# Start slots of the last two scans and the spacing of the first expert weights in a linear attention and two-MoE kernel

## The chip, the cores and the metric

The kernel runs on one core of one Trainium2 chip. The metric is the device time of one execution in microseconds (us). Engines are named TensorE (PE in the profile, PEld for its weight loads), VectorE (DVE), ScalarE (ACT), GpSimd (POOL) and SyncE (SP, which issues the plain DMAs).

## What is computed

Three stages follow each other. In the reference (cut to its core):

```python
for t in range(S):
    state = alpha[:, :, t, :, None] * state + einsum('bhd,bhe->bhde', k[:, :, t], v[:, :, t])
    y[:, :, t] = einsum('bhd,bhde->bhe', q[:, :, t], state)
x = y.transpose(0, 2, 1, 3).reshape(B * S, H * D)          # 3072 tokens x 384
h = x @ w_in;  x = maximum(0.01 * h, h) @ w_out            # 384 -> 2048 -> 384
expert = argmax(x @ w_gate, 1)                             # one of 8 experts for each token
out[t] = gate_prob[t] * (maximum(x[t] @ w1[expert[t]], 0) @ w2[expert[t]])
```

Here B = 4, H = 8, S = 768 and D = 48. The expert weights w1 and w2 are 8 x 384 x 1024 and 8 x 1024 x 384 in float32.

## The kernel before

**Units.** The 3072 tokens are worked on in NU = 8 units of UT = 384 tokens. For a unit, the attention makes the tile xT (the tokens' activations, turned, as a float16 high part and low part), and `moe1` runs the first MoE layer on it. The attention of unit u runs beside `moe1` of units u-2 and u-1.

**Slots.** From unit 1 on the order of the instructions on all engines is written out by hand. `moe1(u)` is a generator that yields 34 times for a unit. Each yield is a slot. In its first half there are 16 slots, one for each block f of 128 hidden columns: nine matmuls (L824), a scaled copy on ScalarE (L833), the leaky maximum on VectorE (L834), the high half on ScalarE (L839) and the low half on GpSimd (L840). In its second half there are 18 slots, mostly of nine matmuls (L847) each. `state["at"]` holds u + f/40 in the first half and u + 0.5 in the second. After each slot `run_slots` steps a list of side generators, and a side generator that yields w is stepped again w slots later.

**Side generators.** They stand in this order, and the instructions of a slot are issued in this order too:

- `full_tiles` (in the last unit alone): the routing of unit 6, then the table of the first NA = 14 expert tiles (`tile_table`, VectorE, L1010 to L1072), then a loop over j that issues the gather of tile j (an indirect DMA from GpSimd, L1303) and turns tile j - LAG (six transposes, L1316, and one ScalarE copy to XT, L1317). LAG is 6.
- `fronts`: for each unit from 2 on, `front`: transposes of alpha (L316), copies to the tile Ft (L521), six levels of a scan along the time axis (L541, two VectorE multiplications for each level), logarithms and exponentials, and the scaled k and q (L578). A start value of `state["at"]` for each unit sets when it begins: units 2 to 5 begin at slot 12 of the unit two before, unit 6 at slot 7 of unit 4, and unit 7 at slot 0 of unit 5.
- `backs`: `back(u)` follows when `front(u)` and `back(u-1)` are done: scores (L675), states (L654), outputs (L703 and L711), xh (L726) and the transposes to xT (L731). For units 2 and 7 its argument `fast` makes two of its pauses shorter.
- `first_weights`: after the last `back`, the attention's memory is given up and the expert weights of the first of four phases are loaded.
- `routed(u)`: the routing of unit u in the second half of unit u+1: small VectorE operations (L941 to L963), two matmuls (L966, L967) and three scatters of the rows (L990).

**Weight pieces.** `load_phase` splits a phase into 16 pieces of 384 KB, w1 and w2 of eight experts in turn. A piece comes by one DMA (L1100) into one of RING = 3 buffers wr. For phase 0, ScalarE squares it (L189, for a check of the range), VectorE rounds it to float16 (L1120) and then makes the low half (L1078). For phase 1, the rounding is done by ScalarE (L1118). A buffer is free when the low half is made, and then the transfer of the third piece after it is issued. The first unit's experts need all w1 pieces of phase 0. Phase 1 puts its w1 into the memory of w_in, so its first eight pieces can be written from the second half of the last unit on, and the rest follows beside the experts.

**After unit 7.** `stage(0)` and `stage(1)` copy an expert's w1 on VectorE (L1342), and then the expert steps begin (L1371, L1397).

Of the kernel before, what the change touches and what calls it, by code (L numbers as in the profile page):

```python
# [29 lines left out]
NU = NTOK // UT  # L30
# [19 lines left out]
C2 = C1 / (2.0 * SW * SW)  # L50
EXPM = 0x7F800000
RING = 3
LAG = 6
AHEAD = (0, 0, 0)
AHEAD2 = 3
WARM = (45,2,2,6,4)
# [17 lines left out]
def tile_kernel(ctx, tc, q, k, v, alpha, w_in, w_out, w_gate, w1, w2, out):  # L74
# [72 lines left out]
    parts, at = [], 2 * P  # L147
# [37 lines left out]
    def squares(src, scrap, scale=1.0):  # L185

        i = sq_n[0]
        sq_n[0] += 1
        A.activation(scrap, src, AF.Square, scale=scale, accum_out=g_sq[:, i : i + 1])  # L189
# [81 lines left out]
    state = {"S": None, "SU": None, "e": None, "nat": 0, "sm": 0, "wo": 0, "half": -1, "turned": -1, "at": 0, "attn": 1, "front": 1}  # L271
# [804 lines left out]
    def after(f):  # L1076

        f() if late is None else late.append(f)  # L1078

    def place(ph):  # L1080

        W1 = wi.tile([P, 2, E, 3, FQ], F16, tag="wi", name="W1") if ph % 2 else pw.tile([P, 2, E, 3, FQ], F16, name="W1")
        Wp[ph] = [W1, None]

    def load_phase(ph, pieces):

        raws = []
        NP = len(pieces)

        def start(n):  # L1090
            e, which = pieces[n]
            raw = pw.tile([P, 2 * DM], F32, tag="wr", name="wr", bufs=RING)
            f0 = ph * FQ
            if which == 0:
                raw = raw.rearrange("p (k f) -> p k f", k=3)
                src = w1[e, :, f0 : f0 + FQ].rearrange("(k p) f -> p k f", p=P)
            else:
                raw = raw.rearrange("p (i d) -> p i d", i=2)
                src = w2[e, f0 : f0 + FQ, :].rearrange("(i p) d -> p i d", p=P)
            nc.sync.dma_start(out=raw, in_=src)  # L1100
            raws.append(raw)

        def scaled(n):
            if n < NP and ph >= 2:
                G.tensor_scalar(raws[n], raws[n], SW, 1.0, ALU.mult, ALU.mult)  # L1105

        for n in range(min(RING, NP)):
            start(n)
        scaled(0)
        for n in range(NP):  # L1110
            scaled(n + 1)
            yield 0.0
            e, which = pieces[n]
            raw, hi, lo = raws[n], *(Wp[ph][which][:, a, e] for a in range(2))
            if ph < 2:
                squares(raw, lo.bitcast(BF16), SW)
                if ph:
                    A.activation(hi, raw, AF.Copy, scale=SW)  # L1118
                else:
                    V.tensor_scalar(hi, raw, SW, None, ALU.mult)  # L1120
                after(partial(V.scalar_tensor_tensor, lo, raw, SW, hi, ALU.mult, ALU.subtract))
            else:
                A.copy(hi, raw)
                squares(raw, lo.bitcast(BF16))
                G.tensor_tensor(out=lo, in0=raw, in1=hi, op=ALU.subtract)  # L1125
            if n + RING < NP:
                start(n + RING)
            yield 1.4
# [99 lines left out]

    def fronts():
        for u in range(2, NU):  # L1230
            while state["at"] < u - 2 + (12, 12, 12, 12, 12, 12, 7, 0)[u] / 40:
                yield 1
            yield from first_front if u == 2 else front(u, False)
            state["front"] = u
            yield 1
# [16 lines left out]
    ALL = [(e, which) for e in range(E) for which in range(2)]  # L1252
# [3 lines left out]
    def first_weights():  # L1256

        nonlocal pw
        while state["attn"] < NU - 1:
            yield 1  # L1260
        pl_ctx.close()
        pa_ctx.close()
        pw = pw_ctx.enter_context(tc.tile_pool(name="pw", bufs=1, side="right", reuse_waits="tile"))
        XT.extend(pw.tile([P, 2, 3, P], F16, name=f"XT{j}") for j in range(NA))
        acc.extend(pw.tile([P, XR], F32, name=f"acc{j}") for j in range(NA))
        sth.extend(pw.tile([P, 2, 3, FQ], F16, name=f"st{i}") for i in range(2))
        place(0)
        Wp[0][1] = pw.tile([P, 2, E, 2, DM], F16, name="W2")
        n = 0
        for _ in load_phase(0, ALL):  # L1270
            n += 1
            if n == 1:
                yield 2
            if n % 2 == 0:
                yield 1
        while state["at"] < NU - 0.5:
            yield 1
        place(1)
        for n, _ in enumerate(load_phase(1, ALL[0::2])):
            yield 1 - n % 2  # L1280

    halves = fronts(), backs()
    sides = [[0, g] for g in (*halves, first_weights())]

    def attention_done(u):
# [26 lines left out]
    def turn(j):  # L1312
        px = pst("a").bitcast(F16)
        x16 = acc[j][:, 0:DM].bitcast(F16)
        for kk in range(6):
            T.transpose(px[:, kk * P : (kk + 1) * P], x16[:, kk * P : (kk + 1) * P], ident16)  # L1316
        A.copy(XT[j].rearrange("p a k t -> p (a k t)"), px[:, 0 : 2 * DM])  # L1317

    def full_tiles():
# [4 lines left out]
        yield 1  # L1324
        for j in range(NA + LAG):
            if j < NA:
                gather(j)
                reg(V, j)
            if j >= LAG:
                turn(j - LAG)  # L1330
            yield 1
# [3 lines left out]
    def reg(eng, j):  # L1335
        if (eng, j) not in regs:
            regs[eng, j] = eng.value_load(ej[0:1, j : j + 1], min_val=0, max_val=E - 1)
        return regs[eng, j]
# [416 lines left out]
```

## Time and profile before

| | |
|---|---|
| median of 3 runs | 891.19 us (889.4 to 894.12) |
| the profiled execution | 887.91 us |
| its span | 885.8 us, mean granted clock 0.972 |
| TensorE busy | 815.1 us (92%) |
| VectorE busy | 636.7 us (72%) |
| ScalarE busy | 515.9 us (58%) |
| GpSimd busy | 466.5 us (53%) |
| chain that ended last | PE 60%, DVE 11%, ACT 8%, issue 3% |

The page gives for each engine its busy time and share of the span, and the chain of work that ended last, followed back from the last instruction. TensorE is the engine with the highest share. The eight units can be found in the trace by the first L824 after the last L847 of the unit before: unit 1 begins at 158.94 us, unit 2 at 231.88, unit 3 at 295.12, unit 4 at 358.79, unit 5 at 435.11, unit 6 at 515.90, unit 7 at 578.60, and the experts' first matmul (L1371) at 638.69.

### The profile page before, as it was taken

The page shows a single profiled execution, that of the slowest core. Times are in us where ns is not written, and L with a number is a line of the kernel's source. Part 1 is how long each engine was busy: PE and PEld are TensorE (multiplying, and loading weights), DVE is VectorE, ACT ScalarE, POOL GpSimd, SP SyncE. Part 2 cuts the span into 40 slices and gives each one's busy share as a digit, 9 for nine tenths or more (in the row PEclk, how much of TensorE's full clock was granted, in tenths as well). Part 3 has the DMA queues.
Part 4 walks back from the last instruction along what each step waited for, and adds up shares of the span by engine and source line. Part 5 has one row for each costly group of instructions (what it writes and reads, how often), then busy time and mean ns, then how long its engine had stood idle before and what let it go on. Part 6 is the DMA issues. An engine that isn't in the chain of part 4 may idle for free.

```text
span 885.8 us, 19845 instructions
## 1 busy us (share of the span) xinstructions
PE 815.1 (92%) x7099; PEld 582.4 (66%) x7099; DVE 636.7 (72%) x1561; ACT 515.9 (58%) x1262; POOL 466.5 (53%) x511
## 2 busy tenths in 40 slices
PE   7887899989999999988997999698899999999995
PEld 4654577666776776665664675454668777777884
DVE  8899886649558559558467658846476888787774
ACT  5657666566475485465266357345838666566343
POOL 6577852454373563563364435246535078678454
PEclk9889999999999999999998999799999999999999
DMA  9654361220211222311000004603614224232121
GB/s 250 174 139 108 102 159 46 54 54 25 58 28 46 63 43 60 62 28 32 24 2 0 28 19 133 193 27 103 189 48 126 91 91 126 92 126 90 66 90 66
DMA packets 130632, 72.21 MB, mean 82 GB/s; under 512 B 102954, under 2 KB 123526, under 8 KB 130528
## 3 DMA queue, kind: packets, MB, share of 16 engines
q1 hardware_dynamic: 125376, 56.64, 24.3%
q0 software_dynamic: 5152, 14.23, 4.7%
q8 instruction: 61, 1.00, 0.5%
q14 instruction: 43, 0.35, 0.1%
HBM read 62.17 MB, written 10.25 MB: 82 GB/s over the span
## 4 chain that ended last, share of the span: by engine, by line
PE 60%; DVE 11%; ACT 8%; issue 3%; POOL 1%; DMA 1%; POOLq 0%; DVEq 0%; ACTq 0%
PE m L847 14%; PE a L1371 12%; PE m L824 12%; PE m L1397 11%; DVE Ft L541 2%; PE a L316 2%; PE a L675 2%; DVE gf L834 2%; PE a L654 2%; ACT gf L833 2%; DVE W L1078 1%; PE a L703 1%; ACT sm L695 1%; ACT W L189 1%; PE a L627 1%
## 5 line engine op out<-in xcount | busy, mean ns | idle before, releaser
L847 PE MATMUL m<-woh,gh 128*128 128x392 f16 x1152 | 210.1, 335 | 1.1 <-POOL gh L840 0.8
L824 PE MATMUL m<-xT,wih 128*128 128x384 f16 x1152 | 203.9, 331 | 2.8 <-DVE gf L834 2.8
L840 POOL TENSOR_TENSOR gh<-gf,gh 128x384 f16<-128x384 f32 x128 | 124.8, 981 | 123.2 <-ACT gh L839 107.1
L847 PEld LDWEIGHTS <-gh 128*128 128x128 f16 x1152 | 113.6, 100 | 74.3 <-issue 5.3
L824 PEld LDWEIGHTS <-wih 128*128 128x128 f16 x1152 | 113.0, 100 | 74.5 <-issue 8.3
L834 DVE SCALAR_TENSOR_TENSOR gf<-m,gf 128x384 f32<-128x384 f32 x128 | 70.8, 554 | 99.2 <-ACT gf L833 98.8
L1371 PE MATMUL a<-XT,st 128*128 128x128 f16 x2016 | 132.4, 220 | 8.1 <-DVE st L1342 7.6
L1371 PEld LDWEIGHTS <-st 128*128 128x128 f16 x2016 | 121.2, 99 | 24.6 <-DVE st L1342 14.4
L1397 PE MATMUL m<-W,hs 128*128 x672 | 127.2, 326 | 0.0
L833 ACT ACTIVATE gf<-m 128x384 f32<-128x384 f32 x128 | 62.4, 489 | 64.7 <-PE m L824 62.9
L839 ACT CAST gh<-gf 128x384 f16<-128x384 f32 x128 | 65.4, 511 | 53.2 <-DVE gf L834 52.0
L1397 PEld LDWEIGHTS <-hs 128*128 128x128 f16 x672 | 61.2, 98 | 29.2
L1342 DVE COPY st<-W 128x1536 f16 x112 | 73.1, 653 | 6.6 <-POOL W L1125 4.3
L1379 ACT ACTIVATE hs<-a 128x256 f16<-128x256 f32 x112 | 42.6, 381 | 59.7 <-PE a L1371 58.6
L1383 DVE SCALAR_TENSOR_TENSOR hs<-a,hs 128x256 f16<-128x256 f32 x112 | 47.2, 422 | 36.9 <-ACT hs L1379 36.5
L990 POOL DMA_INDIRECT x_rows<-xg,pi x24 | 29.0, 1208 | 78.0 <-DVE xg L984 23.6
L1125 POOL TENSOR_TENSOR W<-wr,W 128x768 f16<-128x768 f32 x32 | 53.4, 1670 | 26.0 <-ACT W L189 19.6
L189 ACT ACTIVATE W<-wr 128x768 bf16<-128x768 f32 x64 | 54.0, 844 | 7.8 <-DMA wr<-in_moe_w 7.7
L1412 DVE SCALAR_TENSOR_TENSOR acc<-m,acc 128x384 f32<-128x384 f32 x84 | 51.7, 615 | 6.8 <-PE m L1397 0.7
L316 PE MATMUL a<-ident,nat 128*128 128x128 f32 x288 | 44.6, 289 | 9.5 <-DMA nat<-in_alpha 4.5
L1105 POOL TENSOR_SCALAR wr<-wr 128x768 f32<-128x768 f32 x32 | 33.6, 1050 | 28.7 <-DMA wr<-in_moe_w 28.5
L690 POOL TENSOR_TENSOR sh<-sm,sh 128x512 f16<-128x512 f32 x36 | 44.6, 1260 | 7.3 <-ACT sh L686 7.2
(262 smaller groups left out, 1405.2 us busy)
## 6 DMA issues: line engine op xcount, KB each, us to landing
wr<-in_moe_w SPq DMA_DIRECT2D x64, 384.0 KB, 3.1
raw_in<-in_moe_w_in SPq DMA_DIRECT2D x12, 512.0 KB, 4.3
raw<-in_moe_w_out SPq DMA_DIRECT2D x16, 384.0 KB, 3.6
nat<-in_alpha SPq DMA_DIRECT2D x24, 192.0 KB, 3.5
nat<-in_k SPq DMA_DIRECT2D x24, 192.0 KB, 3.4
nat<-in_q SPq DMA_DIRECT2D x24, 192.0 KB, 3.5
vt<-in_v SPq DMA_DIRECT2D x24, 192.0 KB, 3.7
acc<-x_rows,off POOLq DMA_INDIRECT x28, 3.5
```

The source lines that it names most:

```text
L189: A.activation(scrap, src, AF.Square, scale=scale, accum_out=g_sq[:, i : i + 1])
L316: T.transpose(pt[:, c * P : (c + 1) * P], nt[:, c, pr].rearrange("p z d -> p (z d)"), ident)
L824: T.matmul(ph[:, 0:UT], wih[:, a, kk, f * P : (f + 1) * P], xT[:, b, kk, :], start=(n == 0), stop=(n == 8),)
L833: A.activation(gf, ph[:, 0:UT], AF.Copy, scale=0.01 * CG)
L834: V.scalar_tensor_tensor(gf, ph[:, 0:UT], CG, gf, ALU.mult, ALU.max)
L839: A.copy(g[f][:, 0], gf)
L840: G.tensor_tensor(out=g[f][:, 1], in0=gf, in1=g[f][:, 0], op=ALU.subtract)
L847: T.matmul(po[:, 0:ROW], g[f][:, a, c * P : (c + 1) * P], woh[:, b, f, :], start=(n == 0), stop=(n == 3 * NF - 1),)
L1125: G.tensor_tensor(out=lo, in0=raw, in1=hi, op=ALU.subtract)
L1342: V.tensor_copy(out=sth[i % 2].rearrange("p a k f -> p a (k f)"), in_=Wp[ph][0][:, :, ds(reg(V, j), 1), :, :].rearrange("p a e k f -> p a ...
L1371: T.matmul(hp[:, f * P : (f + 1) * P], st[:, a, kk, f * P : (f + 1) * P], XT[j][:, b, kk, :], start=(n == 0), stop=(n == 8),)
L1397: T.matmul(yp[:, 0:DM], hs[:, a, i, :], W2[:, b, ds(rp, 1), i, :].rearrange("p e f -> p (e f)"), start=(n == 0), stop=(n == 5),)
```

## The change

```diff
@@ -50,7 +50,7 @@
-LAG = 6
+LAG = 5
@@ def fronts():
         for u in range(2, NU):
-            while state["at"] < u - 2 + (12, 12, 12, 12, 12, 12, 7, 0)[u] / 40:
+            while state["at"] < u - 1.7:
                 yield 1
@@ def first_weights():
-        n = 0
-        for _ in load_phase(0, ALL):
-            n += 1
-            if n == 1:
+        for n, _ in enumerate(load_phase(0, ALL)):
+            if n == 0:
                 yield 2
-            if n % 2 == 0:
-                yield 1
+            elif n % 2 == 0:
+                yield 1 if n % 4 or state["at"] > NU - 0.5 else 2
+                while NU - 1 <= state["at"] < NU - 0.9:
+                    yield 1
+                if state["at"] < NU - 0.5 and state["at"] > NU - 1:
+                    yield 3
         while state["at"] < NU - 0.5:
             yield 1
         place(1)
         for n, _ in enumerate(load_phase(1, ALL[0::2])):
-            yield 1 - n % 2
+            if n % 2:
+                yield 1 + (n % 8 == 7)
```

`front` of units 6 and 7 now begins at slot 12 of units 4 and 5, as for the other units. `back(7)` therefore ends at slot 20 of unit 6 and not at slot 8, and the first weight piece is worked on at slot 22 of unit 6 and not at slot 10. The pieces of phase 0 came one for each slot, at slots 10 to 25 of unit 6. Now eight come in slots 22 to 32 of unit 6, two for each three slots. Two come in the first half of unit 7, at slots 7 and 11, and six at its slots 16 to 23. The eight pieces of phase 1 came in slots 17 to 31 of unit 7, one for each two slots. Now they come in slots 23 to 31, one for each slot with one slot left out. The turn of a tile comes five slots after its gather, so that the last turn falls into the last slot of unit 7. No instruction is added or taken away, but for the order.

How the order moves, at three places. First VectorE in unit 5, around its scan (Ft is the tile that L541 scans, gf the leaky maximum of the first half, sm the scores). Before:

```order
L834 SCALAR_TENSOR_TENSOR gf<-m,gf 128x384
L541 TENSOR_TENSOR Ft<-Ft 128x12x32 x2
L681 COPY_PREDICATED sm_116<-tri,a 128x512
L681 COPY_PREDICATED sm_118<-tri,a 128x512
L834 SCALAR_TENSOR_TENSOR gf<-m,gf 128x384
L541 TENSOR_TENSOR Ft<-Ft 128x12x16x2 x2
L834 SCALAR_TENSOR_TENSOR gf<-m,gf 128x384
L541 TENSOR_TENSOR Ft<-Ft 128x12x8x4 x2
L834 SCALAR_TENSOR_TENSOR gf<-m,gf 128x384
L541 TENSOR_TENSOR Ft<-Ft 128x12x4x8 x2
```

and with the change, where the last L834 of unit 5 stands first:

```order
L834 SCALAR_TENSOR_TENSOR gf<-m,gf 128x384
L522 COPY a_5763<-a 128x3 x2
L541 TENSOR_TENSOR Ft<-Ft 128x12x32 x2
L719 TENSOR_REDUCE g_y<-a 128x1
L1512 TENSOR_SCALAR g_al<-g_al 128x64
L257 TENSOR_SCALAR n1m<-g_y 128x1
L1525 TENSOR_REDUCE mins<-g_al 128x1
L261 TENSOR_SCALAR n1s<-n1m 128x1
L262 TENSOR_SCALAR n1e<-n1m 128x1
L541 TENSOR_TENSOR Ft<-Ft 128x12x16x2 x2
L739 TENSOR_TENSOR xT<-a,xT 128x3x128
```

The levels of the scan stood between the L834 of the first half, and they now stand behind all of them, in the second half. With the change, VectorE's and GpSimd's orders in unit 4 are row for row those of unit 2, and in unit 5 those of unit 3, but for six small operations of a check (L1512 and the like) that were elsewhere before.

Then VectorE in unit 6, around the routing of unit 5 (W are the float16 weights, rm, rd, rsx and rex the routing's small tiles). Before:

```order
L1120 TENSOR_SCALAR W_6681<-wr 128x768
L1078 SCALAR_TENSOR_TENSOR W_6681<-wr,W_6681 128x768
L1120 TENSOR_SCALAR W_6680<-wr 128x768
L1078 SCALAR_TENSOR_TENSOR W_6680<-wr,W_6680 128x768
L941 TENSOR_REDUCE rm<-L 128x3
L943 TENSOR_TENSOR rd<-L,rm 128x24
L1120 TENSOR_SCALAR W_6681<-wr 128x768
L1078 SCALAR_TENSOR_TENSOR W_6681<-wr,W_6681 128x768
L948 TENSOR_REDUCE rsx<-rex 128x3
```

and with the change, from the end of the routing's first part to the first piece:

```order
L960 COPY rex<-con 128x8
L961 TENSOR_TENSOR rex<-rex,oh 128x8
L962 TENSOR_TENSOR rex<-rex,oh 128x8
L963 TENSOR_TENSOR con<-rex,oh 128x8
L739 TENSOR_TENSOR xT<-a,xT 128x3x128
L912 TENSOR_REDUCE mx<-m 128x1
L257 TENSOR_SCALAR n2m<-mx 128x1
L261 TENSOR_SCALAR n2s<-n2m 128x1
L262 TENSOR_SCALAR n2e<-n2m 128x1
L914 TENSOR_SCALAR L<-m,n1e 128x8
L915 SCALAR_TENSOR_TENSOR gsc<-n1e,n2e 128x1
L1120 TENSOR_SCALAR W_6864<-wr 128x768
```

The routing's operations stood between the pieces, and they now stand ahead of the first piece.

Last, ScalarE in unit 7, from the last high half (L839) on (XT are the turned tiles, L1320 is the former L1317). Before, with the pieces of phase 1 alone:

```order
L839 CAST gh<-gf 128x384
L189 ACTIVATE W_7480,g_sq<-wr 128x768
L1118 ACTIVATE W_7480<-wr 128x768
L189 ACTIVATE W_7480,g_sq<-wr 128x768
L1118 ACTIVATE W_7480<-wr 128x768
L1317 COPY XT_6650<-a 128x768
L189 ACTIVATE W_7480,g_sq<-wr 128x768
L1118 ACTIVATE W_7480<-wr 128x768
L1317 COPY XT_6651<-a 128x768
```

and with the change:

```order
L839 CAST gh<-gf 128x384
L189 ACTIVATE W_6864,g_sq<-wr 128x768
L189 ACTIVATE W_6865,g_sq<-wr 128x768
L189 ACTIVATE W_6864,g_sq<-wr 128x768
L1320 COPY XT_6834<-a 128x768
L189 ACTIVATE W_6865,g_sq<-wr 128x768
L1320 COPY XT_6835<-a 128x768
L1320 COPY XT_6836<-a 128x768
L189 ACTIVATE W_6864,g_sq<-wr 128x768
L919 ACTIVATE xg<-m,n2s 128x384
L1320 COPY XT_6837<-a 128x768
L189 ACTIVATE W_6865,g_sq<-wr 128x768
```

Six pieces of phase 0 now stand ahead of the eight of phase 1, so ScalarE has 14 pieces, 14 copies to XT and two more operations (L919) in this half where it had eight pieces.

## Rows read from the trace of the kernel before

**Rows 1.** Windows by unit: us, TensorE busy (count), granted clock, DMA share, GB/s
```profile
231.88:295.12 63.24, 63.24 (x508) 1.00 0.22 48
295.12:358.79 63.67, 63.67 (x511) 1.00 0.22 48
358.79:435.11 76.32, 70.40 (x547) 0.98 0.15 32
435.11:515.90 80.79, 72.24 (x571) 0.96 0.02 8
515.90:578.60 62.70, 53.55 (x366) 0.92 0.41 130
578.60:638.69 60.09, 54.03 (x379) 1.00 0.33 103
```
**Rows 2.** Waits of TensorE in unit 5: us in total, times, longest
```profile
PE a L316 <- DVE kt L578: 3.2, 1, 3.2
```
**Rows 3.** VectorE's scan by line: unit 3, then 4 (busy, mean ns)
```profile
L541 DVE TENSOR_TENSOR Ft<-Ft 128x384 f32<-128x384 f32 x12 | 6.1, 559 | 0.0
...
L541 DVE TENSOR_TENSOR Ft<-Ft 128x384 f32<-128x384 f32 x12 | 9.8, 868 | 0.0
```
**Rows 4.** Timeline of VectorE in unit 6, then of TensorE [idle before <-releaser]
```profile
555.88 0.96 DVE L1078 SCALAR_TENSOR_TENSOR W<-wr,W 128x768 f16<-128x768 f32 x1 [0.41 <-ACT W L189]
556.76 0.17 DVE L941 TENSOR_REDUCE rm<-L 128x3 f32<-128x24 f32 x1
...
560.58 0.59 PE L966 MATMUL a<-oh,con 128*128 128x24 f32 x2 [9.15 <-DVE rex L960]
```
**Rows 5.** Timeline of TensorE, end of unit 2: start, us, instruction
```profile
290.54 0.82 PE L316 MATMUL a<-ident,nat 128*128 128x128 f32 x6
291.20 3.65 PE L847 MATMUL m<-woh,gh 128*128 128x392 f16 x21
294.68 0.60 PE L627 MATMUL a<-ident,kt 128*128 128x128 f32 x4
295.12 1.63 PE L824 MATMUL m<-xT,wih 128*128 128x384 f16 x9
```
**Rows 6.** Line L1100, the weight pieces' transfers: unit 6, then unit 7
```profile
L1100 SPq DMA_DIRECT2D wr<-in_moe_w x16: 367/368/368, 539.4 to 572.9; - x16
...
DMA to landing us min/median/max: 2.9/3.6/5.0
...
DMA to landing us min/median/max: 3.1/3.6/4.9
```
**Rows 7.** Timeline of TensorE in unit 1, where back runs fast
```profile
218.49 0.55 PE L731 MATMUL a<-ident,xh 128*128 128x128 f32 x3 [1.66 <-ACT xh L726]
```
**Rows 8.** Timeline of ScalarE in unit 7, second half
```profile
611.50 0.84 ACT L189 ACTIVATE W<-wr 128x768 bf16<-128x768 f32 x1
...
612.34 0.83 ACT L1118 ACTIVATE W<-wr 128x768 f16<-128x768 f32 x1
613.07 0.83 ACT L189 ACTIVATE W<-wr 128x768 bf16<-128x768 f32 x1
...
614.73 0.80 ACT L1317 COPY XT<-a 128x768 f16<-128x768 f16 x1
615.42 0.85 ACT L189 ACTIVATE W<-wr 128x768 bf16<-128x768 f32 x1
```
**Rows 9.** Timeline of ScalarE, then of TensorE, end of unit 7
```profile
635.82 0.86 ACT L1118 ACTIVATE W<-wr 128x768 f16<-128x768 f32 x1
...
638.69 3.69 PE L1371 MATMUL a<-XT,st 128*128 128x128 f16 x36 [2.27 <-DVE st L1342]
```
**Rows 10.** Waits of TensorE in unit 7: us in total, times, longest
```profile
PE a L1316 <- DMA acc<-x_rows,off: 1.9, 2, 1.0
```
**Rows 11.** Timeline of VectorE, then of GpSimd, table of tiles in unit 7
```profile
602.00 2.59 DVE L1021 COPY ten<-tnt 128x8 f32<-128x8 f32 x1
...
601.90 2.65 POOL L840 TENSOR_TENSOR gh<-gf,gh 128x384 f16<-128x384 f32 x3
```

## The prediction

> **What bounds the kernel now.** I read the windows by unit first. Units 2 and 3 take 63.24 and 63.67 us, and TensorE is busy in all of it, at a granted clock of 1.00. Unit 4 takes 76.32 us, unit 5 takes 80.79 and unit 6 takes 62.70; TensorE is idle for 5.9, 8.6 and 9.2 us of them, and the granted clock is 0.98, 0.96 and 0.92 [rows 1]. So TensorE is the bound, and what can be won lies where it waits or runs at the lower of its two levels.
>
> The waits say on whom it waits. In unit 5 it waits 3.2 us on VectorE's scaling of k in a front [rows 2]. The groups by line show what makes VectorE late there: the twelve scan operations take 6.1 us in unit 3 and 9.8 in unit 4, 559 against 868 ns for one [rows 3]. In unit 6 the timeline shows one wait of 9.15 us for the routing, whose operations on VectorE stand behind the weight pieces (the piece ahead of L941 ends at 556.7) [rows 4].
>
> **Units 4 and 5.** With the change, VectorE and GpSimd have the rows of unit 2 in unit 4 and those of unit 3 in unit 5, and the attention work on TensorE is theirs too. I take their times: 63.24 for 76.32 and 63.67 for 80.79, together -30.2 us. A part of this is work that moves into unit 6 and is counted there. The bounds: no better than units 2 and 3, which have no idle time left; at worst the waits stay, which is the second rival.
>
> **Unit 6.** Against unit 2, the new unit 6 has the same TensorE work but for the 36 alpha, k and q transposes and four of the k turns. Six transposes take 0.66 us to the next row (290.54 to 291.20), so 36 take 3.96; the four turns take 0.44 [rows 5]. So unit 6 becomes 63.24 - 3.96 - 0.44 = 58.84, which is -3.9. This needs the 9.15 us wait to go, and the routing now stands ahead of the first piece. The eight pieces that follow have two for three slots of nine matmuls, which is 2.25 us for one (21 take 3.48 us there, 291.20 to 294.68, so nine take 1.5). In the run shown, 16 transfers were issued between 539.4 and 572.9, 2.2 us apart, while each waited for its buffer [rows 6], so the pieces can hold this pace. I cost them at nothing: in the second half, ScalarE and VectorE have no L833 and L834 to deliver. Were that cover gone, each would take 0.84 us of ScalarE from them (below), and from VectorE 0.96 for the low half [rows 4] and somewhat less for the rounding, some 1.5. `back(7)` runs fast here, and where `back(2)` did so, TensorE waited 1.66 us for xh [rows 7]; I take 0, since VectorE has no front beside it, and keep 1.7 for the range.
>
> Units 4 to 6 together: 219.8 before, 185.75 now, **-34.1 us**.
>
> **Unit 7.** Here the change costs. Its first half gets two pieces, 0.84 us of ScalarE and 1.5 of VectorE each. I cost them at nothing on TensorE, whose products run ahead of both by up to four buffers, but they stand ahead of the tile table on VectorE, and I add 0.4 us for the gathers that wait on it. In the second half ScalarE becomes the bound. After its last L839 a piece of phase 0 takes 0.84 us, a piece of phase 1 takes 613.07 - 611.50 = 1.57, and a copy to XT takes 615.42 - 614.73 = 0.69 [rows 8]. Up to the end of the last piece stand six, eight and twelve of these and two L919, which are smaller than a copy to XT and taken as 0.5: 5.0 + 12.6 + 8.3 + 1.0 = 26.9 us. From 611.50 this ends at 638.4. It ended at 636.55 so far (635.82, and 0.73 until the next can start), and the first expert matmul came 2.1 us later, after a wait of 2.27 on VectorE's copy of the weights [rows 9]. That is +1.9 with no wait in it.
>
> The waits of ScalarE: the first copy to XT can't come before 614.73, and three pieces end at 614.0, so 0.7. The fourth piece needs the buffer of the first, which is free at about 613.3 (611.50 + 0.84 + 0.96 for the low half); its transfer lands 3.1 to 4.9 later [rows 6], so at 616.4 to 618.2, and ScalarE is there at 615.4: 1.0 to 2.8, and I take 2.1, since the gathers run beside it. The copies of the second and third tile wait for gathers, as TensorE does now for 1.9 us in all [rows 10], and with LAG 5 TensorE comes one slot sooner: 1.0. For the ring later on I take 0.4: three services of 1.57 + 0.69 are 6.8 us, and a buffer comes back after 3.6 to 4.9 + 1.57 + 0.96, 6.1 to 7.4. Together 4.2, and unit 7 costs 1.9 + 4.2 + 0.4 = **+6.5 us**. The bounds are +1.9 (no wait) and about +13 (each transfer 4.9, 0.6 for each of the later pieces, and 3 for the table). TensorE's own longer waits at the first turns lie beside ScalarE's work, which ends last. I leave the experts as they are: their instructions and their late pieces are the same.
>
> **The sum.** 887.9 - 34.1 + 6.5 = 860.3 us against the profiled execution. That execution lies 3.3 us under the median of the runs shown (891.2), so in their terms the forecast is **864 us**.
>
> **A rule against this change.** The scan operations are slower where GpSimd has L840 to do, and in unit 7 a VectorE copy of eight elements took 2.59 us, while GpSimd ran three L840 in 2.65 [rows 11]. The Trainium skill (SBUF — State Buffer, Terms) says that VectorE and GpSimd share one pair of ports, which one of them holds for a whole instruction while the other is blocked. By that rule the two pieces in the first half of unit 7 are slowed by L840 and slow it. It would give the first rival's 867 in place of 864. The trace agrees on the copy of 2.59 us. For the scans it speaks for the change, as they now stand where no L840 runs.
>
> **The rivals.**
>
> First, the ports or the transfers hold unit 7. Either the table of tiles slips by some 3 us behind the two pieces, two of whose operations double, as the copy in [rows 11] did. Or each transfer takes 4.9 us beside the gathers, as the longest did [rows 6]. Unit 7 then costs +9.5 to +13: 867 to 870 in terms of the median. For it speaks that 14 pieces and 14 gathers now fall into one half; against it, that the median landing is 3.6 in either unit. The Trainium skill (Trainium Kernel Development and Optimization, Key Constraints) has the queues of SyncE and GpSimd on the same 16 DMA engines, interleaved; the landing times are as that lets one expect.
>
> Second, the waits of units 4 and 5 come with the work and not with its slots, so that the change doesn't do there what its order says. Then only unit 6's wait goes: 887.9 - 9.15 + 6.5 = 885.2, or 888.5 by the median. Against it speaks that units 2 and 3 do the same work in these slots without a wait [rows 1].
>
> Third, it is slower: the ring of three buffers gives no overlap in the second half of unit 7, and the 14 pieces come one after the other. With 4.9 + 1.57 + 0.96 = 7.4 us for each they take 104 us, where the half took 35, so +69 for -34: 926 us by the median. It decides from a pace of (35 + 34) / 14 = 4.9 us for each piece. The 2.2 us of unit 6 speak against it [rows 6].
>
> **How the numbers follow.** The forecast gets 0.80, the first rival 0.12, the second 0.06 and the third 0.02. Half a per cent, 4.5 us, is about what a measurement of this kernel can tell from no change. The second rival's 888.5 lies within it. So faster is 0.80 + 0.12 = 0.92, the same 0.06 and slower 0.02. The range begins at 855, where unit 7 costs +1.9 and the runs lie 1 to 3 us over the profile (859), less 4 for the spread of runs (889.4 to 894.12). It ends at 876: the first rival's 870, 1.7 for the fast `back(7)` and 4 for the same spread. It leaves out the second and third rivals.
>
> **What would show it.** In the profile of the changed kernel: units 4 and 5 of about 63.5 us each with no wait of TensorE over 0.5 us and a clock of 1.00, and scan operations of 0.56 us; unit 6 of 59 us without the wait on L960; unit 7 of some 66 us, in whose second half ScalarE is busy nearly throughout, and a wait of 5 to 8 us ahead of the first expert matmul; 247 us from there to the end. The prediction is wrong if the scans still take over 0.8 us for one, if TensorE waits for the routing, or if the first expert matmul comes over 72 us after unit 7 began.

## The result, and the profile after

| | before | changed |
|---|---|---|
| median | 890.4 us (889.4 to 894.12, 4 runs) | 866.58 us (865.69 to 870.18, 4 runs) |
| ratio | | 0.9743, 95% interval 0.9712 to 0.9773 |
| the profiled execution | 887.91 us, span 885.8 | 870.18 us, span 868.2 |
| TensorE busy | 815.1 us (92%) | 808.8 us (93%) |
| ScalarE busy | 515.9 us | 514.5 us |
| chain that ended last | PE 60%, DVE 11%, ACT 8% | PE 66%, DVE 8%, ACT 5% |

The change saves 23.8 us of median; 864 was forecast. The profiled execution of the changed kernel is the longest of its four, and 4.9 us of its span are lost before unit 2 begins (at 236.80 and not at 231.88), where both programs are the same. So I compare stretch by stretch.

Windows by unit of the changed kernel, units 4 to 7 and then the experts (us, TensorE busy with its count, granted clock, DMA share, GB/s), against [rows 1]:

```profile
363.70:426.94 63.24, 63.24 (x508) 1.00 0.18 39
426.94:490.61 63.67, 63.67 (x511) 1.00 0.03 11
490.61:549.48 58.87, 58.87 (x468) 1.00 0.22 69
549.48:620.36 70.88, 55.50 (x379) 0.94 0.45 145
620.36:868.20 247.84, 232.94 (x2782) 0.98 0.29 92
```

Units 4, 5 and 6 have no idle time of TensorE left: 185.78 us for 219.81, which is -34.0. Unit 7 takes 70.88 for 60.09, +10.8. The experts take 247.84 for 247.11, +0.7. The sum is -22.5, and with the 4.9 of the start -17.6, the difference of the spans.

The scan of unit 4 by line, against [rows 3]:

```profile
L541 DVE TENSOR_TENSOR Ft<-Ft 128x384 f32<-128x384 f32 x12 | 6.1, 560 | 0.0
```

It was 9.8 us, at 868 ns for one. Two pairs of scan operations in unit 4 of the kernel before, and what GpSimd does beside the first (L690 makes the low half of the scores):

```profile
392.68 1.98 DVE L541 TENSOR_TENSOR Ft<-Ft 128x384 f32<-128x384 f32 x2
...
398.56 1.02 DVE L541 TENSOR_TENSOR Ft<-Ft 128x384 f32<-128x384 f32 x2
...
392.73 2.95 POOL L690 TENSOR_TENSOR sh<-sm,sh 128x512 f16<-128x512 f32 x2
```

The pair at 398.56, with GpSimd idle, takes 1.02 us, as the pairs of unit 3 do. The slowest pairs, here and in unit 5 (1.98 and 2.23 us in each), stand beside L690, which the prediction does not name, and L840 follows it. The slower operations are 3.7 us of what unit 4 loses.

What the change costs lies in unit 7. Its two halves, cut where the last L839 has ended, of the kernel before (here and below where every engine is shown: us, then busy with count of PE, PEld, DVE, ACT and POOL, then granted clock, DMA share, GB/s):

```profile
578.60:611.50 32.90, 32.05 (x196) 19.06 (x194) 20.89 (x67) 15.02 (x35) 17.66 (x22) 1.00 0.05 19
611.50:638.69 27.19, 21.98 (x183) 14.13 (x184) 11.82 (x24) 23.73 (x41) 17.73 (x27) 1.00 0.66 204
```

and of the changed kernel:

```profile
549.48:585.89 36.41, 32.21 (x196) 19.05 (x194) 25.70 (x74) 17.38 (x41) 18.65 (x22) 1.00 0.20 65
585.89:620.36 34.47, 23.29 (x183) 15.05 (x183) 20.98 (x36) 28.88 (x53) 19.38 (x27) 0.87 0.72 229
```

The first half has grown by 3.5 us and the second by 7.3. TensorE's work is nearly the same in both (32.2 and 23.3 us). VectorE has 4.8 us more in the first half, ScalarE 5.2 more in the second.

**First half.** The timeline of VectorE in the kernel before: the L834 on either side of three gaps, between which the routing and the table stand:

```profile
593.22 0.56 DVE L834 SCALAR_TENSOR_TENSOR gf<-m,gf 128x384 f32<-128x384 f32 x1 [0.82 <-ACT gf L833]
...
595.43 0.54 DVE L834 SCALAR_TENSOR_TENSOR gf<-m,gf 128x384 f32<-128x384 f32 x1
...
600.00 0.56 DVE L834 SCALAR_TENSOR_TENSOR gf<-m,gf 128x384 f32<-128x384 f32 x1 [0.97 <-ACT gf L833]
...
601.52 0.56 DVE L834 SCALAR_TENSOR_TENSOR gf<-m,gf 128x384 f32<-128x384 f32 x1 [0.69 <-ACT gf L833]
...
606.47 0.55 DVE L834 SCALAR_TENSOR_TENSOR gf<-m,gf 128x384 f32<-128x384 f32 x1
```

and the same three gaps in the changed kernel, where the two pieces (L1120 and L1078) stand in the first and the second:

```profile
564.92 0.56 DVE L834 SCALAR_TENSOR_TENSOR gf<-m,gf 128x384 f32<-128x384 f32 x1 [0.82 <-ACT gf L833]
...
566.29 1.22 DVE L1120 TENSOR_SCALAR W<-wr 128x768 f16<-128x768 f32 x1
567.62 0.96 DVE L1078 SCALAR_TENSOR_TENSOR W<-wr,W 128x768 f16<-128x768 f32 x1
568.50 0.55 DVE L834 SCALAR_TENSOR_TENSOR gf<-m,gf 128x384 f32<-128x384 f32 x1
...
573.06 0.56 DVE L834 SCALAR_TENSOR_TENSOR gf<-m,gf 128x384 f32<-128x384 f32 x1 [0.97 <-ACT gf L833]
...
573.73 2.47 DVE L1012 CAST tnt<-tni 128x8 f32<-128x8 int32 x1
576.12 0.55 DVE L1120 TENSOR_SCALAR W<-wr 128x768 f16<-128x768 f32 x1
576.77 0.96 DVE L1078 SCALAR_TENSOR_TENSOR W<-wr,W 128x768 f16<-128x768 f32 x1
577.65 0.55 DVE L834 SCALAR_TENSOR_TENSOR gf<-m,gf 128x384 f32<-128x384 f32 x1
578.11 0.16 DVE L1021 COPY ten<-tnt 128x8 f32<-128x8 f32 x1
...
580.86 0.55 DVE L834 SCALAR_TENSOR_TENSOR gf<-m,gf 128x384 f32<-128x384 f32 x1
```

The timeline of ScalarE beside it, in the changed kernel:

```profile
562.88 0.49 ACT L833 ACTIVATE gf<-m 128x384 f32<-128x384 f32 x1
563.99 0.51 ACT L839 CAST gh<-gf 128x384 f16<-128x384 f32 x1 [0.62 <-DVE gf L834]
564.40 0.48 ACT L833 ACTIVATE gf<-m 128x384 f32<-128x384 f32 x1
...
569.08 0.51 ACT L839 CAST gh<-gf 128x384 f16<-128x384 f32 x1 [2.58 <-DVE gf L834]
```

These rows show that VectorE and ScalarE wait for each other in turn. An L833 follows its L839 without a wait, the L839 waits 0.62 us for VectorE's L834, and the next L834 waits 0.97 for the L833. One round takes 1.52 us (600.00 to 601.52). A gap of VectorE holds 0.97 us of other work for nothing, and what is longer pushes every later round. From L834 to L834 the first gap is 3.58 us where it was 2.21, the second 4.59 where it was 1.52, and the third 3.21 where it was 4.95, since the long operation (L1021 so far, [rows 11]) now is L1012 in the gap before. That is +1.4, +3.1 and -1.7, together 2.7. In these gaps the two pieces would take 3.0 us (0.55 and 0.96 for each), and VectorE's slowed operations come to 0.6 us more than before: +0.7 for the rounding of 1.22, +2.3 for the cast, -2.4 for L1021, and, in rows not shown, +0.7 for L1023 (2.02 for 1.32) and -0.6 for L982 (0.17 for 0.79). The idle time that this fills was 0.9. The other 0.8 of the 3.5 stand at the unit's start, where the last piece of unit 6 comes late: the first L834 is 3.1 us after the start (552.55) and was 2.2 (580.85).

**Second half.** The timeline of ScalarE in the changed kernel: first its waits, last its last piece, against [rows 8] and [rows 9]:

```profile
585.89 0.84 ACT L189 ACTIVATE W<-wr 128x768 bf16<-128x768 f32 x1
...
589.01 0.80 ACT L1320 COPY XT<-a 128x768 f16<-128x768 f16 x1 [0.54 <-PE a L1319]
592.35 0.84 ACT L189 ACTIVATE W<-wr 128x768 bf16<-128x768 f32 x1 [2.54 <-DMA wr<-in_moe_w]
...
594.72 0.80 ACT L1320 COPY XT<-a 128x768 f16<-128x768 f16 x1 [0.74 <-PE a L1319]
...
599.20 0.84 ACT L189 ACTIVATE W<-wr 128x768 bf16<-128x768 f32 x1 [0.86 <-DMA wr<-in_moe_w]
...
618.00 0.84 ACT L1118 ACTIVATE W<-wr 128x768 f16<-128x768 f32 x1
```

and of TensorE, its longer wait on a gather (the other is 1.20) and its wait ahead of the experts, against [rows 10] and [rows 9]:

```profile
588.47 0.51 PE L1319 MATMUL a<-ident,acc 128*128 128x128 f16 x6 [2.60 <-DMA acc<-x_rows,off]
...
620.36 5.53 PE L1374 MATMUL a<-XT,st 128*128 128x128 f16 x54 [7.04 <-DVE st L1345]
```

ScalarE's waits are 0.54, 2.54, 0.74 and 0.86, and later 0.61 (604.42) and 0.16 (606.94), 5.45 us in all. From 585.89 to the end of the last piece at 618.74 are 32.85, so its work is 27.4. TensorE had been done 7 us before the first expert matmul.

### The profile page after: what moved, and what is told of

The parts are those of the page before. It is cut to its first block, busy times and chain, and to the rows that moved or that the text cites. A ratio compares the mean times of both kernels' runs of the same rounds, so it can differ in the third digit from the quotient of the medians.

```text
span 868.2 us, 19865 instructions
## 1 busy us (share of the span) xinstructions
PE 808.8 (93%) x7099; PEld 582.5 (67%) x7099; DVE 627.5 (72%) x1561; ACT 514.5 (59%) x1262; POOL 466.0 (54%) x511
## 4 chain that ended last, share of the span: by engine, by line
PE 66%; DVE 8%; ACT 5%; DMA 3%; issue 2%; POOL 0%; DVEq 0%; SPq 0%; ACTq 0%; POOLq 0%
PE m L824 16%; PE m L847 14%; PE a L1374 12%; PE m L1400 11%; DMA wr<-in_moe_w 3%; PE a L316 3%; PE a L675 2%; PE a L654 2%; PE a L703 1%; DVE W L1078 1%; PE a L711 1%; ACT W L189 1%; DVE gf L834 1%; DVE st L1345 1%; DVE Ft L541 1%
## 5 line engine op out<-in xcount | busy, mean ns | idle before, releaser
L847 PE MATMUL m<-woh,gh 128*128 128x392 f16 x1152 | 206.1, 332 | 2.8 <-DVE gf L834 2.6
L840 POOL TENSOR_TENSOR gh<-gf,gh 128x384 f16<-128x384 f32 x128 | 120.1, 945 | 110.3 <-ACT gh L839 86.4
L847 PEld LDWEIGHTS <-gh 128*128 128x128 f16 x1152 | 113.1, 99 | 73.8 <-issue 5.3
L834 DVE SCALAR_TENSOR_TENSOR gf<-m,gf 128x384 f32<-128x384 f32 x128 | 71.0, 556 | 103.4 <-ACT gf L833 102.8
L1374 PE MATMUL a<-XT,st 128*128 128x128 f16 x2016 | 133.1, 221 | 13.1 <-DVE st L1345 12.6
L833 ACT ACTIVATE gf<-m 128x384 f32<-128x384 f32 x128 | 62.4, 488 | 61.7 <-PE m L824 60.2
L839 ACT CAST gh<-gf 128x384 f16<-128x384 f32 x128 | 65.5, 511 | 49.9 <-DVE gf L834 48.3
L990 POOL DMA_INDIRECT x_rows<-xg,pi x24 | 32.2, 1340 | 80.5 <-DVE xg L984 47.3
L1421 POOL DMA_INDIRECT out<-acc x28 | 28.9, 1031 | 29.8 <-DVE acc L1415 29.2
```

The source lines that it names most:

```text
L833: A.activation(gf, ph[:, 0:UT], AF.Copy, scale=0.01 * CG)
L834: V.scalar_tensor_tensor(gf, ph[:, 0:UT], CG, gf, ALU.mult, ALU.max)
L839: A.copy(g[f][:, 0], gf)
L840: G.tensor_tensor(out=g[f][:, 1], in0=gf, in1=g[f][:, 0], op=ALU.subtract)
L847: T.matmul(po[:, 0:ROW], g[f][:, a, c * P : (c + 1) * P], woh[:, b, f, :], start=(n == 0), stop=(n == 3 * NF - 1),)
L1374: T.matmul(hp[:, f * P : (f + 1) * P], st[:, a, kk, f * P : (f + 1) * P], XT[j][:, b, kk, :], start=(n == 0), stop=(n == 8),)
```

## The experiments

Eight of the twelve runs were made on one chip, where the kernel before took 890.45 and 891.85 us. The other four (eight late, four buffers, both, all three) were made on another, where it took 909.23, and where TensorE shows waits named "issue" of up to 2.2 us for one at about 640 to 656 us. Of those four I therefore compare units, not totals; units 4 to 6 take 185.8 us there too. The changed kernel itself was not run there, so what these four show of unit 7 assumes that it takes the same time on either. Ratios are against the kernel before, with a 95% interval.

### Which part brings the gain

**Scans alone**, on the kernel before:

```diff
-            while state["at"] < u - 2 + (12, 12, 12, 12, 12, 12, 7, 0)[u] / 40:
+            while state["at"] < u - 1.7:
```

> The kernel before with the start of the scans alone changed (slot 12 of units 4 and 5); the lag of six and the pieces' spacing as before, so that 13 pieces come one for each slot at the end of unit 6 and three in the first slots of unit 7. Theory (the gain is the scans', the price is unit 7's pieces): units 4 and 5 of 63.5 us each without a TensorE wait over 0.5 us, unit 6 of 59 to 61, unit 7 of 62 to 65 (its second half has eight pieces, as before, and not 14, but the three pieces at its start delay the table), 857 to 864 us in all. Rival 1 (the scans' waits come with the work): units 4 and 5 of 76 and 81, 885 or more. Rival 2 (the spacing is needed too): the pieces at one for each slot outrun their transfers, 2.2 us apart, and hold TensorE at the seam of units 6 and 7, 867 to 875.

Measured: 869.66 us, ratio 0.9767 (0.9732 to 0.9801). Units 4 and 6 take 63.24 and 58.86 us. Windows of units 5 and 7, then TensorE's longest wait in unit 7:

```profile
424.88:488.55 63.67, 63.67 (x512) 1.00 0.03 11
...
547.41:620.23 72.82, 57.24 (x380) 0.93 0.43 139
```

```profile
558.67 4.47 PE L824 MATMUL m<-xT,wih 128*128 128x384 f16 x18 [6.71 <-DVE gf L834]
```

All of the 34 us come from the start slots of the scans. My figure for unit 7 (62 to 65) was wrong: the second rival came about. VectorE has five pieces ahead of its first L834, which comes 10.7 us after unit 7 began (558.06), and TensorE runs out of buffers.

**Weights and lag alone**, on the changed kernel: the tuple of start slots put back (the diff above the other way round).

> The changed kernel with the old start slots of the scans, so that only the spacing of the pieces and the lag are new (four pieces in the first half of unit 6, twelve in its second). Theory: units 4 and 5 of 76 and 81 us as before, with the wait on the scaled k in unit 5 and scans of over 0.8 us in unit 4; unit 6 between 59 and 64, since the pieces still stand ahead of the routing but less closely; 882 to 891 in all. Rival (the gain comes from the pieces' spacing): 865 to 872.

Measured: 886.66 us, 0.9956 (0.9938 to 0.9975), as the theory has it. Windows of units 4, 5 and 6:

```profile
360.02:436.35 76.33, 69.96 (x547) 0.98 0.15 32
436.35:517.73 81.38, 71.39 (x572) 0.96 0.02 8
517.73:577.08 59.35, 54.09 (x366) 0.94 0.39 124
```

The wait for the routing in unit 6 is 5.26 us where it was 9.15 [rows 4]. The spacing and the lag alone are worth 3.8 us, and nearly as much on top of the scans (869.66 against 866.07 and 866.58: 3.1 to 3.6).

**One scan back**, on the changed kernel:

```diff
-            while state["at"] < u - 1.7:
+            while state["at"] < u - 1.7 - (u == 6) * 5 / 40:
```

> The changed kernel with the scan of unit 6 alone back at slot 7 of unit 4, beside the L834 and L840 of that unit's first half; unit 7's stays at slot 12 of unit 5. Theory (each unit's loss is its own scan's, standing beside L834 and L840): unit 4 of 74.5 to 77 us with scan operations of over 0.8 us, unit 5 of 62 to 65 without a wait over 0.5, unit 6 of 59; 11 to 14 us over the changed kernel. Rival (the loss needs both scans out of their slots, or unit 4's loss is not the scan's): unit 4 under 70, 0 to 6 us over the changed kernel.

> The changed kernel itself, run beside the other three on one chip, as their base. On a chip that treats the kernel before as the first one did: 866 to 868 us; units 4, 5 and 6 of 63.2, 63.7 and 58.9 us and unit 7 of 70.5 to 71.3.

Measured: 875.24 us (0.9826, 0.9784 to 0.9867), beside 866.07 of the changed kernel run with it (0.971, 0.9674 to 0.9746; its units 63.23, 63.68, 58.86 and 70.91). Windows of units 4 and 5 with the scan back, and its operations in unit 4:

```profile
359.41:435.76 76.35, 71.00 (x547) 0.96 0.15 32
435.76:495.64 59.88, 59.88 (x472) 1.00 0.03 11
```

```profile
L541 DVE TENSOR_TENSOR Ft<-Ft 128x384 f32<-128x384 f32 x12 | 9.8, 868 | 0.0
```

Unit 4 is back at 76.3 with one scan moved, and the operations are at 868 ns. The theory holds for the place. The total was missed (+9.2, I had 11 to 14), since work moves with the scan: unit 5 falls from 63.67 to 59.88 (472 matmul records for 511). Of the 13.1 us of unit 4, 3.8 are work moved and 9.3 are loss. The slower scan operations make up 3.7 of the 9.3. What makes up the rest was not taken apart, and no run moves GpSimd's work away from a scan.

### What sets the first half of unit 7

**Ten pieces in unit 6**, on the changed kernel:

```diff
-                yield 1 if n % 4 or state["at"] > NU - 0.5 else 2
-                while NU - 1 <= state["at"] < NU - 0.9:
-                    yield 1
-                if state["at"] < NU - 0.5 and state["at"] > NU - 1:
-                    yield 3
+                yield 1
+                while n >= 20 and state["at"] < NU - 0.5:
+                    yield 1
```

> The changed kernel with no piece in the first half of unit 7: ten pieces at one for each slot in unit 6, six in the second half of unit 7 as now. Theory (the two pieces in unit 7's first half push the table and the last L839 by about 3 us): the last L839 ends 33 to 34 us after the unit begins, not 36.4, unit 7 takes 67 to 68.5, 863 to 864.5 us in all. Rival 1 (unit 7's second half is set by gathers and transfers, so an earlier last L839 only waits longer): last L839 earlier, total 866 to 868. Rival 2 (two more pieces in unit 6 outrun their transfers): unit 6 of 60 or more or a longer wait at unit 7's start, 866 to 870.

Measured: 867.17 us (0.9734, 0.9698 to 0.977), unit 7 71.47. The second rival: the pieces outran their transfers, VectorE did three of them after unit 7 had begun, TensorE waited there, and the last L839 ended after 36.9 us. The experiment didn't take the delay away, but moved it.

```profile
556.00 7.55 PE L824 MATMUL m<-xT,wih 128*128 128x384 f16 x36 [2.76 <-DVE gf L834]
```

**Eight late**: as the changed kernel in unit 6, but the two pieces go to the second half.

```diff
-                while NU - 1 <= state["at"] < NU - 0.9:
+                while n >= 16 and state["at"] < NU - 0.5:
                     yield 1
-                if state["at"] < NU - 0.5 and state["at"] > NU - 1:
-                    yield 3
```

> The changed kernel with the two pieces of unit 7's first half moved to its second half, which then has eight of phase 0 and eight of phase 1; unit 6 as in the changed kernel. Theory (the first half goes in step between ScalarE and VectorE, 1.52 us for a slot, so that each us of VectorE work put ahead of the table pushes it by as much): the last L839 ends 33.3 to 34 us after the unit begins and not 36.4. What the second half then takes tells its bound apart: if ScalarE's work alone sets it, the two pieces cost 0.84 us each and unit 7 takes 69 to 70 us, 865 to 866 in all; if the ring of three buffers does, at about 2.4 us for each piece, unit 7 takes 72 to 73.5, 868 to 869.5. Rival for the first half (the table's own operations beside GpSimd push it): the last L839 stays at 36.

Measured: 878.5 us on the other chip (0.9669, 0.9634 to 0.9703). Halves of unit 7:

```profile
545.20:578.88 33.68, 32.39 (x189) 19.05 (x188) 21.27 (x69) 16.04 (x36) 17.66 (x22) 0.95 0.14 48
578.88:618.77 39.89, 23.46 (x193) 14.65 (x190) 23.90 (x40) 30.69 (x57) 19.31 (x27) 0.88 0.68 213
```

The first half is 33.7, as the theory has it: taking the two pieces out brings 2.7 us. How much of this is the pieces' own work is open. With them gone, the slowed operations are 1.6 us less too: L1012 takes 0.17 again, L1023 1.32 and L1021 2.25. The late last piece of unit 6 is still there, with the first L834 2.8 us after the start. With a fourth buffer it goes (next part: 2.2 us to the first L834, and a first half of 35.5 for 36.4). The second half grew by 5.4 us for two pieces, not by 1.7, so ScalarE's work is not all that sets it. Unit 7 as a whole is at the ring's figure (73.57 us, where 72 to 73.5 were expected of it).

### What sets the second half

**Rounding on VectorE**, on the changed kernel:

```diff
-                if ph:
+                if ph and which:
                     A.activation(hi, raw, AF.Copy, scale=SW)
```

> The changed kernel with the rounding of the eight phase 1 pieces of unit 7 on VectorE, not on ScalarE (8 x 0.83 = 6.6 us less on ScalarE, some 0.6 each more on VectorE). Theory (ScalarE's work ends last in unit 7): the wait ahead of the first expert matmul falls from 7.0 us to 1 to 3, the total to 860.5 to 863. Rival (the ring of three buffers and its transfers set the pace of the pieces): ScalarE's waits on transfers grow from 4 us to 8 or more, the wait ahead of the experts stays over 5, 865 to 867.

**Four buffers**, on the changed kernel (the identity of the attention goes to the attention's memory for it, and the branch after the experts makes one of its own):

```diff
-RING = 3
+RING = 4
...
-    ident = cp.tile([P, P], F32, name="ident")
+    ident = pa.tile([P, P], F32, name="ident")
```

> The changed kernel with four buffers for the pieces and not three (the identity of the attention is kept in the attention's memory to make room). Theory (ScalarE's 4.2 us of waits on transfers in unit 7's second half come from the ring, a buffer being free too late): these waits fall under 1.5, the wait ahead of the first expert matmul to 3 to 4 from 7.0, 861.5 to 864 us in all. Rival (the transfers themselves are the limit, beside the gathers): landing times rise from 3.5 to over 4.3, ScalarE waits as long, 865.5 to 867.5.

**Both**:

> Four buffers, and the rounding of the eight phase 1 pieces of unit 7 on VectorE. Theory (two limits stand close together in unit 7's second half, ScalarE's work and the ring; each alone hides behind the other): both gone at once, TensorE's own work and the first gathers set the half, 28 to 30 us from the last L839 to the first expert matmul where the changed kernel has 34.5; 858.5 to 861.5 us, more than the sum of the gains of either alone. Rival (the transfers are the limit): 863 to 866.

Measured: 865.01 us (0.9722, 0.9685 to 0.976) with the rounding moved; on the other chip 875.09 (0.9622, 0.9602 to 0.9643) with four buffers and 872.65 (0.9608, 0.9576 to 0.964) with both. The second half of unit 7 in the three, in this order, each from its own profile:

```profile
581.14:613.75 32.61, 23.22 (x193) 14.76 (x191) 26.42 (x44) 23.37 (x45) 19.86 (x27) 0.95 0.76 237
```

```profile
579.68:613.80 34.12, 23.36 (x184) 14.99 (x184) 20.92 (x36) 28.75 (x53) 19.16 (x27) 0.92 0.73 232
```

```profile
580.63:611.08 30.45, 23.26 (x194) 14.83 (x191) 26.89 (x44) 23.14 (x45) 19.30 (x27) 0.99 0.80 260
```

Against 34.47, taking 5.5 us of work from ScalarE (28.88 to 23.37) brings 1.9, the fourth buffer 0.35, both together 4.0. A second profile of the changed kernel has 34.18 for this half, so the 0.35 can't be told from nothing. With the work moved alone, the experts wait 5.67 us and the total is 865.01, both the rival's; ScalarE waits 6.0 us on transfers where it waited 4.2, less than the rival's 8. With four buffers alone no wait on a transfer is left, but ScalarE now waits for turned tiles, the first of which wait for their gathers (TensorE 2.59 and 1.36 us); the wait ahead of the experts stays at 6.6 where 3 to 4 were expected, and my theory of the ring alone falls. In unit 7 ScalarE's waits on turned tiles grow from 1.3 to 5.2 us. So the limits stand close behind each other, and only with both edits does the half shorten by more than the sum of either. What is left with both seems to be VectorE, busy for 26.9 of the 30.5 us; no run took work from it. Its last rounding took 2.45 us for 0.55, while GpSimd cleared tiles for the last experts (six L1302 and six L1303 from 606.67 to 609.07):

```profile
607.04 2.45 DVE L1120 TENSOR_SCALAR W<-wr 128x768 f16<-128x768 f32 x1
```

**All three** (four buffers, rounding on VectorE, eight late):

> Four buffers, the rounding on VectorE, and no piece in the first half of unit 7 (16 in its second). Theory: the last L839 33 to 33.8 us after the unit begins, and 29 to 31 from there to the first expert matmul, unit 7 of 62 to 65 us; 857 to 860 us in all, the fastest. Rival (16 pieces in one half are too many for transfers of 3.5 us and four buffers): the half takes 34 or more, 861 to 865.

Measured: unit 7 70.85 (874.86 us in all, 0.9621, 0.9587 to 0.9655). The first half was as expected, 32.4, the second 38.4, which is the rival's, though not by its cause: ScalarE waited 0.9 us on one transfer. TensorE was done 10.6 us before the experts, and VectorE did the last pieces one after the other, each 0.55 and 0.96. Sixteen pieces at one for each slot end behind the last slot.

**Lag of six**: `LAG = 6` in the changed kernel.

> The changed kernel with a lag of six between a tile's gather and its turn. Theory (ScalarE ends last in unit 7, and the turns are covered): TensorE's waits on the first gathers, 3.8 us in the changed kernel, fall by 1 to 2, but ScalarE has the same work behind it, so that unit 7 and the total stay within 1 us of the changed kernel. Rival (the first gathers hold the second half): 1.5 to 3 us less.

Measured: 867.35 us (867.04 to 867.69), 1.3 over the changed kernel beside it, unit 7 71.56 for 70.91. TensorE's waits on gathers fell from 4.0 to 3.1 us, but the piece that waits longest (3.5 us) now stands ahead of the first copy to XT. The 1.3 us lie within the intervals (0.9692 to 0.976 against 0.9674 to 0.9746), so all that can be said is that a lag of five was no cost.

**Ten in six with four buffers and the rounding on VectorE**, the edits above together:

> Four buffers, the rounding on VectorE, and ten pieces at one for each slot in unit 6 so that none stands in the first half of unit 7. Theory (the fourth buffer lets the transfers keep one piece a slot, and the table loses its 3 us): unit 6 of 59 to 60 us, the last L839 33 to 34.5 us after unit 7 begins, 30 to 31.5 from there to the first expert matmul, unit 7 of 63 to 65.5; 5 to 8 us under the changed kernel. Rival (the pieces spill into unit 7's start as with three buffers): the last L839 at 36 or later, 3 to 5 us under it.

Measured: 863.13 us (0.9674, 0.964 to 0.9708), 2.9 under the changed kernel run with it (866.07, 0.9674 to 0.9746), with unit 7 at 68.16. The rival came about: pieces still spill into unit 7, and the last L839 ended after 36.25 us. One of its runs is longer than any of the changed kernel (871.56); the other four are 862.27 to 865.62 against 864.84 to 866.95. It has the lowest median that was measured on the first chip, though the intervals overlap. By units, the version with two pieces left in the first half, four buffers and the rounding on VectorE is better, with unit 7 at 65.98; it was not run on that chip.

## Why the prediction was right, and where it was not

| step | predicted | measured |
|---|---|---|
| units 4 and 5 | -30.2 | -30.2 |
| unit 6 | -3.9 | -3.8 |
| unit 7, the table's slip | +0.4 | +3.5 |
| unit 7, second half | +6.1 | +7.3 |
| experts | 0 | +0.7 |
| sum | -27.6 | -22.5 |

**Units 4 to 6** came out to 0.1 us. Taking the new slots' time from units 2 and 3, which do the same work in the same slots, counts work and waits at once. That the scans' place and nothing else does it is shown by the scans alone and by one scan back. How a scan beside the first half costs 9.3 us is known in part only: its operations are 3.7 us slower, beside L690 as well as L840. The second rival (the waits come with the work) is refuted, the third too: transfers overlap in the second half, 14 pieces in 34.5 us. (The 35 us that the third rival gives the half so far count from TensorE's first L847 at 603.74; from the last L839 it was 27.2.)

**The step that failed** is the two pieces in unit 7's first half: "I cost them at nothing on TensorE, whose products run ahead of both by up to four buffers", with 0.4 us for the table. TensorE's lead doesn't matter there. VectorE and ScalarE go in turn, 1.52 us a round with 0.97 free on VectorE, so what a piece of 1.5 us and the operations beside it take beyond the free time pushes the table and the last L839 one for one. Eight late measured it: 2.7 us for two pieces and for the operations that are slow beside them. The working had no term for the free time of a round. The other 0.8 us belong to unit 6, whose eight pieces the prediction cost at nothing too: the last of them ran into unit 7's start.

The first rival had this slip at some 3 us, and its +9.5 to +13 for unit 7 holds the +10.8. Its price came about, its mechanism in part. One rounding took 1.22 for 0.55 us beside an L840, and the second took its usual 0.55. The cast of 2.47 us replaces the copy of 2.59 in [rows 11], which now takes 0.16, so that the long operation changed its place. Together the slowed operations are 0.6 us more than before, but 1.6 more than in eight late. Its other cause, transfers of 4.9 us, did not come about: the median landing of the pieces in that half is 3.7 us, the longest 5.8. The Trainium skill (SBUF — State Buffer, Terms) has VectorE and GpSimd lock one pair of ports for a whole instruction. The trace agrees in part: the cast ends at 576.20, and the two L840 beside it end at 576.16. But the cast began at 573.73, before the first of them (574.38), and waited for both. No run separated the lock from other causes.

**The second half** was right in its mechanism. The work term of 26.9 measured 27.4. ScalarE's waits of 4.2 measured 5.45: the first copy 0.54 for 0.7, the fourth piece 2.54 for 2.1, the gathers 0.74 for 1.0, and the ring 1.6 for 0.4, which is the mis-sized one. From the end of the last piece to the experts it was 1.6 and not 2.1. The claim that "ScalarE becomes the bound" is half of the truth: relieved of 5.5 us, it gave back 1.9, since transfers and gathers stand right behind it. The wait ahead of the first expert matmul was 7.04 us, in the 5 to 8 forecast.

**The experts** took 0.7 more in this profile. After its wait TensorE ran 54 matmuls at a granted clock of 0.56, near the lower of its two levels (1.2 of 2.4 GHz), where the kernel before ran 36 at 0.55. Windows of that stretch, of the kernel before:

```profile
638.69:642.38 3.69, 3.69 (x36) 0.55 0.35 107
```

and of the changed kernel:

```profile
620.36:625.89 5.53, 5.53 (x55) 0.56 0.25 74
```

18 matmuls more at 0.102 us (3.69 / 36), and not at the 0.066 of later ones (18 in 1.18), are 0.66 us. It is not a fixed price of the change. In the second profile of the changed kernel the 54 took 5.07 us after a wait of 6.14, and the experts 247.28, 0.2 us more than before. Nor does the wait alone set it: with the scans alone TensorE waited 2.27 us, as in the kernel before, and ran its 36 in 2.18 us at a clock of 1.00.

**Luck.** The forecast of 864 is only 2.6 us from 866.58, while the stretches add up to a gain 5.1 us smaller than forecast. Of the difference, 0.8 is the median before, now 890.4 and not 891.2. The rest, 1.7, comes from profiled executions that don't lie equally far from their medians, and the working had no hold on that.

## What to carry to other kernels

When work is moved into slots whose twins already run clean, take the twins' time and spend the effort on where the work that it displaces ends up. An engine's idle time covers an added operation only if the idle comes in gaps as long as the operation: look for two engines that release each other in turn, and count the gap of one round. Where relieving one limit brings little, relieve the second with it before giving up either: here 1.9 us and next to nothing made 4.0 together.

## What was not expected of the hardware

The time until unit 2 begins ran from 231.5 to 241.3 us over the profiles. The program up to there is the same but for where the runs with four buffers keep the identity, and both ends are runs with four buffers. The longest run of the last kernel (871.56, against 862.27) is the one with 241.3. Simple operations of VectorE beside GpSimd took 2 to 15 times their usual time (a cast of eight elements 2.47 us for 0.17, a rounding 2.45 for 0.55), and when one got its usual time back, the one before it became long. The second chip's waits named "issue", which no kernel on the first chip shows at that place, were not looked into; their cause is open.
